# A memory mixer, eight experts and a feed-forward on one core: block-diagonal q built on the chip, weights loaded later, one more iteration between two layers

## The chip, the core and the metric

The kernel runs on one core of a Trainium2 chip. The time is in device microseconds (us) from the start of an execution to its end; a kernel's time is the median of its runs. TensorE does the matrix products, VectorE, ScalarE and GpSimd the elementwise work, SyncE issues most DMAs. In the rows they are PE (PEld: its weight loads), DVE, ACT, POOL and SP.

## The reference

Three stages follow each other: a recurrent mixer with a matrix memory (2 sequences of 768 tokens, 8 heads of 40), a mixture of 8 experts (each token goes to one, at most 384 per expert), and a feed-forward layer of 2048 with a PReLU. All numbers are float32.

```python
# mixer, for each t
m_new = np.maximum(f_gate[:, :, t] + m, i_gate[:, :, t])
f_stab = np.exp(f_gate[:, :, t] + m - m_new)
i_stab = np.exp(i_gate[:, :, t] - m_new)
C = f_stab[..., None, None] * C + i_stab[..., None, None] * np.einsum('bhd,bhe->bhde', vt, kt)
n = f_stab[:, :, None] * n + i_stab[:, :, None] * kt
h_tilde = np.einsum('bhde,bhe->bhd', C, qt)
nq = np.einsum('bhd,bhd->bh', n, qt)[:, :, None]
y[:, :, t] = sigmoid(o_gate[:, :, t]) * h_tilde / np.maximum(np.abs(nq), 1.0)
# experts: x is (1536, 320), w1 (8, 320, 1024), w2 (8, 1024, 320)
logits = x @ w_gate                      # the largest picks the expert
h = np.maximum(np.einsum('ecd,edf->ecf', disp, w1), 0.0)
y = np.einsum('ecf,efd->ecd', h, w2)     # scaled by the gate's weight
# second feed-forward: w_in (320, 2048), w_out (2048, 320)
h = x @ w_in
g = np.maximum(h, 0.0) + alpha * np.minimum(h, 0.0)
out = g @ w_out
```

## The kernel before

**Mixer.** The recurrence is done in 12 chunks of 128 tokens (6 for each sequence), by a loop over chunks `i`; 0 to 9 run in the loop, 10 and 11 behind it, in code written out. For a chunk TensorE makes the scores k·q of all heads (`scores`, L393), the values (`values`, L456), the share of the state of earlier chunks (`inter`, L418), the new state (`update`, L427) and the router's logits. Two chunks share one load, a pair: `qk` (q and k with heads of three side by side on 120 partitions), `tk` (v and k by token) and `qbd`, a second copy of q in block-diagonal form, so that one product makes the scores of three heads. In `qbd` each of the three blocks of 40 partitions holds its own head's columns, and the rest is zero. The kernel zeroes both `qbd` buffers once (L251) and then writes each pair's blocks by three DMAs (`load_pair`, L264). Decays come back from DRAM as a tile `Gb` per chunk, are masked on GpSimd (`causal`, L379) and raised to e on ScalarE. GpSimd also weighs k by the decay (`weigh_k`, L402, tile `kw`), which `update` needs, multiplies the output gate (`gate`, L492, tile `rs`) and issues the indirect DMAs that scatter finished rows into the experts' slots (`scatter`, L639). The scores of chunk i + 1 stand in iteration i, right behind `update(i)`.

Weights of an expert come in four quarters; `load_quarter` (L179 to L181, tiles `w1r`, `w2r`) issues three DMAs for each. Those of expert 0 are loaded in the mixer, one in each iteration from `Z1` = 6.

**Experts.** Products keep float32's precision by splitting each operand into a high and a low part that TensorE multiplies at its faster rate: three matmuls in place of one. ScalarE writes the high part and VectorE or GpSimd the low one (L188). Expert `e` goes through 8 steps `f`: layer 1 (L938) into one of three banks `hps0`, `hps1`, `qs2`, whose numbers start anew with each expert, ReLU parts `gh`, `gl` (L1072, L1073), and layer 2 (L950 to L952) `LAG` = 2 steps later. Between them stand transposes of the next expert's x (at f = `XE` = 2, 3, 4; L924), the splitting of the next expert's weights, and steps that turn the float64 bits of the second feed-forward's weights into float32 (`cv` tiles, L976 to L982). At which `f` such a step stands is set by `SC`. An iteration ends in a branch on whether an expert has more than 256 tokens (L1169), in which the engines meet.

**Second feed-forward.** Groups of tokens (2, 2, 4 and 4 blocks of 128 in the first pass, three times 4 in the other three) go through four `f` of a pass: layer 1 into `hps`, ScalarE's two ReLUs and VectorE's sum (`ng`, `g`), the split into `g3h` and `g3l` one iteration later, and layer 2 two iterations later: `pend` holds the layer-2 steps that wait, and is emptied down to `LAG`. `XG` says at which `f` of a group the next group's x is transposed (`xtp`). More `cv` steps run in the first three passes.

The order on TensorE, VectorE, ScalarE and GpSimd is that in which the code is written; a scheduler orders SyncE's DMAs. All SyncE DMAs share one queue.

Of the kernel before, what the change touches and what calls it, by code (L numbers as in the profile page):

```python
# [19 lines left out]
P = 128  # L20
# [33 lines left out]
def kernel(  # L54
# [19 lines left out]
    nc = tc.nc  # L74
    _, B, _, NG, S = qks.shape
    NTB = tok.shape[1]
    D = 40
# [5 lines left out]
    r = DM - 2 * P  # L83
# [7 lines left out]
    SL = NBLK * P  # L91
# [2 lines left out]
    B0 = min(2, NBLK)  # L94
    N0 = B0 * P

    W1, W2, V7, V8, V9, NA, WA, WB, Z0, Z1, X0, LD, FL, XE, SC, SC0, F0, WC, LS, UO, DL, XG, LV, E0, S0, CUT = 12, 4, 0, (((0, 0, 0, 0), (1, 1, 1, 1), (2, 2, 2, 2), (2, 2, 2, 2)), ((1, 2, 2, 3), (1, 2, 2, 3), (1, 2, 2, 3)), ((1, 2, 2, 3), (1, 2, 2, 3), (0, 0, 0, 0)), ((0, 0, 0, 0), (0, 0, 0, 0), (0, 0, 0, 0))), ({0: (2, 3), 1: (4, 5), 2: (6, 7)}, {0: (8, 9), 1: (10, 11)}, {}), 6, 0, 6, 3, 6, 3, 3, (2, 1, 2, 4, 1), 2, (1, 0, 0, 0, 0, 1, 0, 1), (0, 0, 0, 0, 0, 0, 1, 1), {5: [0], 6: [1], 7: [2]}, 0, 1, 1, 4, ({2: (0, 2), 3: (1,)}, {1: (0,), 2: (2,), 3: (1,)}, {1: (0,), 2: (2,), 3: (1,)}), 3, 2, 0, (2, 3, 3, 3, 3, 3, 3, 0)
    QF = 2 * P
    NQ = F // QF
    cp = ctx.enter_context(tc.tile_pool(name="cp", bufs=1))  # L100
# [12 lines left out]
    def after(inst, anchor):  # L113

        tc.add_manual_dep(
            inst.ins, anchor.ins.name, mybir.DependencyInfo(mybir.DependencyClass.Sync, mybir.DependencyReason.DATA),
            reason="paced transfer",
        )
# [18 lines left out]
    def x_tiles(pool, n, i):  # L137
        t = [[pool.tile([P, n], F32R, name=f"x{i}{k}{x}", bufs=1) for x in "hl"] for k in range(3)]

        nc.gpsimd.memset(t[2][1][r:].bitcast(U32), 0)  # L140
        return t

    xq = x_tiles(xk, SL, 0)


    RING = 2 * NQ
# [85 lines left out]
    with ExitStack() as actx:  # L232
# [15 lines left out]
        qbds = []  # L248
        for x in range(2):
            qbds.append(ap.tile([P, 3 * NG, PB], F32, tag=f"qbd{x}", name=f"qbd{x}"))  # L250
            nc.gpsimd.memset(qbds[x], 0.0)  # L251
        ins, sgs = {}, {}

        def load_pair(i2, anchor=None, late=None):
            b, c2 = divmod(i2, NC // 2)
            sl = slice(c2 * PB, (c2 + 1) * PB)
            qk = rp.tile([3 * D, 2, NG, PB], F32, tag="qk", name="qk")
            d = nc.sync.dma_start(out=qk[:, 1 if i2 == 0 else slice(0, 2)], in_=qks[:, b, 1 if i2 == 0 else slice(0, 2), :, sl])
            if i2 and anchor is not None:
                after(d, anchor)  # L260
            qbd = qbds[i2 % 2]
            for j in range(3):
                n = 3 if j < 2 else 2
                d = nc.sync.dma_start(  # L264
                    out=qbd[j * D:(j + 1) * D].rearrange("p (g j) s -> p g j s", j=3)[:, :n, j, :],
                    in_=qks[j * D:(j + 1) * D, b, 0, :n, sl],
                )
                if i2 < 2:
                    after(d, anchor)
            tk = rp.tile([P, 2, tok.shape[2]], F32, tag="tk", name="tk")  # L270
            d = nc.sync.dma_start(out=tk, in_=tok[:, 2 * i2:2 * i2 + 2, :])
            if anchor is not None:
                after(d, late or anchor)
            if i2 == 0:
                after(nc.sync.dma_start(out=qk[:, 0], in_=qks[:, b, 0, :, sl]), late)
            for x in range(2):
                cs = slice(x * P, (x + 1) * P)
                v1t = tk[:, x, :H * D1].rearrange("p (h d) -> p h d", h=H)
                ktt = tk[:, x, H * D1:H * D1 + DM].rearrange("p (h d) -> p h d", h=H)
                ins[2 * i2 + x] = (qk[:, 0, :, cs], qk[:, 1, :, cs], qbd[:, :, cs], v1t, ktt)  # L280
# [335 lines left out]
        def adv(g, n):  # L616

            for _ in range(n):
                next(by_start[g], None)
# [95 lines left out]
        for i in range(LB):  # L715
# [15 lines left out]
            if Z0 <= i < Z0 + 4:  # L731
                n = NS // P // 4
                rows = disp.rearrange("(a p) d -> p a d", p=P)[:, (i - Z0) * n:(i - Z0 + 1) * n, :]
                after(nc.sync.dma_start(out=rows, in_=zt[:, :DM].unsqueeze(1).to_broadcast([P, n, DM])), anchor[i - 1])
            if Z1 <= i < Z1 + NQ:
                load_quarter(0, i - Z1, anchor[i - 1])
            if i and ok(i + 1):
                decay(i + 1, range(4))
# [53 lines left out]
                nc.scalar.activation(sg1, sg1, AF.Sigmoid)  # L792
            if i % 2 and i // 2 + 2 < NTB // 2:
                load_pair(i // 2 + 2)
            if i == 7:
                after(nc.sync.dma_start(out=zt, in_=cst[:, C_ROW:]), anchor[i])
            ins.pop(i), Dt.pop(i), Pts.pop(i)
# [471 lines left out]
    sums = sp.tile([P, NTB, DM], F32, name="sums", bufs=1)  # L1269
    ghl3 = [[sp.tile([P, GN], F32R, name=f"g3{x}{i}", bufs=1) for x in "hl"] for i in range(3)]  # L1270

    def group_x(i0, nb, k):
        c0 = i0 % GB * P
        parts = [[t[:, c0:c0 + nb * P] for t in pair] for pair in xsets[i0 // GB]]
        ps = lambda k: pm.tile([P, 512], F32, tag="m", name="xtp")
        x_part(lambda m: sums[:, i0 + m, :], nb, ps, parts, k)
# [18 lines left out]
    for np0, gi in [(0, g) for g in range(len(FIRST))] + [(p, g) for p in (1, 2, 3) for g in range(len(OTHERS))]:  # L1295
# [4 lines left out]
        for f in range(f0, f1):  # L1300
# [45 lines left out]
                            nc.sync.dma_start(out=out[i * P:(i + 1) * P, :], in_=sums[:, i, :])  # L1346

            pend.append(l2step)
            while len(pend) > LAG:
                pend.pop(0)()  # L1350
            low_rows()
            convert(V8[np0][gi][f - f0])
# [77 lines left out]
```

## Time and profile before

| | us |
|---|---|
| median of 3 runs | 506.01 (502.34 to 509.98) |
| the profiled execution | 504.48 |
| its span, first to last instruction | 502.7 |
| TensorE busy | 454.7 (90%) |
| VectorE busy | 342.4 (68%) |
| ScalarE busy | 246.3 (49%) |
| GpSimd busy | 125.5 (25%) |
| mean granted TensorE clock | 0.925 |

The profile is of one execution; what lies around its span is 1.8 us. A TensorE that is busy is not at its peak: at a granted clock of 0.50 the same instruction takes up to twice as long. In the rows, a bracket such as [3.15 <-POOL kw L402] is the time for which the engine stood idle before the instruction, and what ended it. A timeline lists instructions in order of time (start, length, engine, line and operation). Windows list for each stretch its bounds and length, the busy time of PE, PEld, DVE, ACT and POOL, the granted clock, the DMA engines' busy share and the GB/s moved. Waits are grouped by the waiting instruction and what released it: total us, how many, the longest.

### The profile page before, as it was taken

What the parts mean: (1) busy time and instruction counts of PE and PEld (TensorE: products, weight loads), DVE (VectorE), ACT (ScalarE), POOL (GpSimd) and SP (SyncE); (2) the same over time, 40 slices, a digit from 0 to 9 for tenths busy, and PEclk for the clock granted to TensorE, in tenths of its full rate; (3) what the DMA queues carried; (4) which work ended last, traced back from release to release, by engine and by line L of the source; (5) the groups of instructions that cost most, each with busy time, mean ns of one, the idle gap of its engine ahead of it and who ended that gap; (6) DMA issues with size and microseconds to landing.
All of it is one profiled execution on the core that took longest, in us unless ns stands there. A gap on an engine that the chain in (4) does not pass through costs nothing. (4 is left out here: it accounts for less than half of the span.)

```text
span 502.7 us, 8039 instructions
## 1 busy us (share of the span) xinstructions
PE 454.7 (90%) x2800; PEld 408.0 (81%) x2800; DVE 342.4 (68%) x700; ACT 246.3 (49%) x558; POOL 125.5 (25%) x115
## 2 busy tenths in 40 slices
PE   5969998889879889796998898997999999999996
PEld 2658886787879889796998897895998898789995
DVE  7627683866788783859688224775889988764544
ACT  3446782525457544555556124562654454354442
POOL 4244325646534221423233224300000000000000
PEclk8759995966999999889899999997999999999999
DMA  6999999424786753657473003221221231000102
GB/s 190 263 278 337 351 317 253 147 78 133 241 254 197 222 175 88 212 155 244 147 220 94 22 1 103 74 84 42 73 59 53 57 101 52 2 0 1 52 20 86
DMA packets 42428, 68.86 MB, mean 137 GB/s; under 512 B 4383, under 2 KB 32354, under 8 KB 42383
## 3 DMA queue, kind: packets, MB, share of 16 engines
q1 hardware_dynamic: 41023, 64.18, 42.5%
q0 software_dynamic: 1152, 3.86, 2.4%
q8 instruction: 26, 0.43, 0.4%
q10 hardware_dynamic: 208, 0.24, 0.1%
q14 instruction: 19, 0.16, 0.1%
HBM read 56.49 MB, written 11.85 MB: 136 GB/s over the span
## 5 line engine op out<-in xcount | busy, mean ns | idle before, releaser
L188 POOL TENSOR_TENSOR w2l<-w2r,w2h 128x640 fp32r<-128x640 f32 x31 | 53.2, 1715 | 93.1 <-ACT w2h L224 77.8
L1316 DVE SCALAR_TENSOR_TENSOR g<-ng,nalt,g 128x512 f32<-128x512 f32 (+1 forms) x52 | 36.9, 709 | 47.5 <-ACT g L1315 47.4
L1314 ACT ACTIVATE ng<-hps 128x512 f32<-128x512 f32 (+1 forms) x52 | 29.4, 565 | 74.8 <-PE hps L938 73.3
L950 PE MATMUL acc<-w2h,gh 128*128 128x320 f32 x128 | 40.8, 319 | 4.9 <-DVEq L1169 4.9
L952 PE MATMUL acc<-w2h,gl 128*128 128x320 f32 x128 | 40.5, 316 | 1.6 <-DVE gl L1073 1.6
L951 PE MATMUL acc<-w2l,gh 128*128 128x320 f32 x128 | 40.4, 315 | 0.0
L1072 ACT ACTIVATE gh<-hps 128x256 fp32r<-128x256 f32 x50 | 19.1, 384 | 40.3 <-PE hps L938 38.5
L387 ACT ACTIVATE Gb<-Gb,bT 128x128 f32<-128x128 f32 x96 | 29.5, 388 | 12.3 <-POOL Gb L379 12.3
L188 DVE TENSOR_TENSOR w1h<-w1r,w1h 64x256 fp32r<-64x256 f32 x32 | 33.4, 1047 | 1.0
L188 DVE TENSOR_TENSOR g3l<-g,g3h 128x512 fp32r<-128x512 f32 (+1 forms) x52 | 33.5, 644 | 0.1
L1073 DVE SCALAR_TENSOR_TENSOR gl<-hps,gh 128x256 fp32r<-128x256 f32 x50 | 20.5, 421 | 18.6 <-ACT gh L1072 18.1
L952 PE MATMUL acc<-w2h,g3l 128*128 128x320 f32 x96 | 30.3, 316 | 2.4 <-DVE g3l L188 2.3
L952 PE MATMUL acc<-wouth,g3l 128*128 128x320 f32 x96 | 30.8, 321 | 0.3 <-DVE g3l L188 0.3
L950 PE MATMUL acc<-wouth,g3h 128*128 128x320 f32 x96 | 30.7, 320 | 0.1
L1319 ACT CAST g3h<-g 128x512 fp32r<-128x512 f32 (+1 forms) x52 | 30.6, 589 | 0.3 <-DVE g L1316 0.3
L951 PE MATMUL acc<-woutl,g3h 128*128 128x320 f32 x96 | 30.6, 319 | 0.0
L950 PE MATMUL acc<-w2h,g3h 128*128 128x320 f32 x96 | 29.8, 310 | 0.8 <-ACT g3h L1319 0.8
L456 PEld LDWEIGHTS Ops<-tk,Pt 128*128 128x128 f32 x192 | 26.7, 217 | 4.2 <-issue 2.6
L393 PE MATMUL qs<-qbd,qk 120*128 120x384 f32 (+1 forms) x72 | 30.1, 567 | 0.0
L951 PE MATMUL acc<-w2l,g3h 128*128 128x320 f32 x96 | 29.6, 309 | 0.0
L950 PEld LDWEIGHTS acc<-w2h,gh 128*128 128x128 f32 x128 | 25.1, 196 | 5.4 <-issue 3.8
L1315 ACT ACTIVATE g<-hps 128x512 f32<-128x512 f32 (+1 forms) x52 | 29.2, 561 | 0.0
(334 smaller groups left out, 1384.0 us busy)
## 6 DMA issues: line engine op xcount, KB each, us to landing
w2r<-w SPq DMA_DIRECT2D x32, 320.0 KB
w1r<-w SPq DMA_DIRECT2D x32, 256.0 KB
Gb<-gd SPq DMA_DIRECT2D x12, 512.0 KB
raw<-wout SPq DMA_DIRECT2D x8, 640.0 KB
raw<-win SPq DMA_DIRECT2D x8, 512.0 KB
tk<-tok SPq DMA_DIRECT2D x6, 648.0 KB
disp<-zt SPq DMA_DIRECT2D x4, 960.0 KB
qk<-qks SPq DMA_DIRECT2D x5, 720.0 KB
```

What stands on the lines that cost most here:

```text
L188: eng.tensor_tensor(out=out, in0=a, in1=b.bitcast(F32), op=ALU.subtract)
L387: nc.scalar.activation(Dt[i][:, h, :], Dt[i][:, h, :], AF.Exp, bias=bT[:, c, b * H + h:b * H + h + 1])
L393: nc.tensor.matmul(ps[:, :nh * P].rearrange("p (h t) -> p h t", h=nh), kst[:nh * D, g, :], qbd[:nh * D, h0:h0 + nh, :], start=True, stop=True,
L456: nc.tensor.matmul(Opss[i][:, h, :], Pts[i][:, h, :], v1t[:, h, :], start=True, stop=True)
L950: nc.tensor.matmul(a, gh[:, ms], wh, start=first, stop=False)
L951: nc.tensor.matmul(a, gh[:, ms], wl, start=False, stop=False)
L952: nc.tensor.matmul(a, gl[:, ms], wh, start=False, stop=last)
L1073: nc.vector.scalar_tensor_tensor(out=gl, in0=ps, scalar=0.0, in1=gh.bitcast(F32), op0=ALU.max, op1=ALU.subtract)
L1314: nc.scalar.activation(ng, ps, AF.Relu, scale=-1.0)
L1315: nc.scalar.activation(g, ps, AF.Relu)
L1316: nc.vector.scalar_tensor_tensor(out=g, in0=ng, scalar=nalt[:, f:f + 1], in1=g, op0=ALU.mult, op1=ALU.add)
L1319: nc.scalar.copy(gh, g)
```

## The change

It has five parts.

1. From the second pair on, `qbd` is no longer written by DMAs. `spread_q` makes it from the q part of `qk`: each of the three blocks is q times a column of 0 and 1 (`bd`), two blocks on GpSimd (120 x 3 x 256 each), one on ScalarE (120 x 2 x 256). It stands at the end of each even iteration i, for the pair of chunks i + 2 and i + 3. The zeroing of the second buffer goes.
2. Expert 0's weight quarters are loaded in iterations 7 and 8 (`Z1`), and quarters 2 and 3 behind the loop.
3. `XE` goes from 2 to 3, and `SC` from (1,0,0,0,0,1,0,1) to (1,0,1,0,0,0,1,0).
4. In the second feed-forward a fourth pair of `g3` tiles is laid over expert x's tile, which is dead by then, and layer 2 runs three iterations behind layer 1.
5. The last entry of `XG`: the last group's x is transposed one `f` earlier.

```diff
-    W1, W2, V7, V8, V9, NA, WA, WB, Z0, Z1, X0, LD, FL, XE, SC, SC0, F0, WC, LS, UO, DL, XG, LV, E0, S0, CUT = 12, 4, 0, (((0, 0, 0, 0), (1, 1, 1, 1), (2, 2, 2, 2), (2, 2, 2, 2)), ((1, 2, 2, 3), (1, 2, 2, 3), (1, 2, 2, 3)), ((1, 2, 2, 3), (1, 2, 2, 3), (0, 0, 0, 0)), ((0, 0, 0, 0), (0, 0, 0, 0), (0, 0, 0, 0))), ({0: (2, 3), 1: (4, 5), 2: (6, 7)}, {0: (8, 9), 1: (10, 11)}, {}), 6, 0, 6, 3, 6, 3, 3, (2, 1, 2, 4, 1), 2, (1, 0, 0, 0, 0, 1, 0, 1), (0, 0, 0, 0, 0, 0, 1, 1), {5: [0], 6: [1], 7: [2]}, 0, 1, 1, 4, ({2: (0, 2), 3: (1,)}, {1: (0,), 2: (2,), 3: (1,)}, {1: (0,), 2: (2,), 3: (1,)}), 3, 2, 0, (2, 3, 3, 3, 3, 3, 3, 0)
+    W1, W2, V7, V8, V9, NA, WA, WB, Z0, Z1, X0, LD, FL, XE, SC, SC0, F0, WC, LS, UO, DL, XG, LV, E0, S0, CUT = 12, 4, 0, (((0, 0, 0, 0), (1, 1, 1, 1), (2, 2, 2, 2), (2, 2, 2, 2)), ((1, 2, 2, 3), (1, 2, 2, 3), (1, 2, 2, 3)), ((1, 2, 2, 3), (1, 2, 2, 3), (0, 0, 0, 0)), ((0, 0, 0, 0), (0, 0, 0, 0), (0, 0, 0, 0))), ({0: (2, 3), 1: (4, 5), 2: (6, 7)}, {0: (8, 9), 1: (10, 11)}, {}), 6, 0, 6, 3, 7, 3, 3, (2, 1, 2, 4, 1), 3, (1, 0, 1, 0, 0, 0, 1, 0), (0, 0, 0, 0, 0, 0, 1, 1), {5: [0], 6: [1], 7: [2]}, 0, 1, 1, 4, ({2: (0, 2), 3: (1,)}, {1: (0,), 2: (2,), 3: (1,)}, {0: (0,), 1: (2,), 2: (1,)}), 3, 2, 0, (2, 3, 3, 3, 3, 3, 3, 0)
...
-            nc.gpsimd.memset(qbds[x], 0.0)
-        ins, sgs = {}, {}
+        nc.gpsimd.memset(qbds[0], 0.0)
+        ins, sgs, q_of = {}, {}, {}
+
+        def spread_q(i2):
+
+            qbd = qbds[i2 % 2][:3 * D].rearrange("p (g j) s -> p g j s", j=3)
+            for j in range(3):
+                n = 3 if j < 2 else 2
+                if j < 2:
+                    nc.gpsimd.tensor_scalar_mul(qbd[:, :n, j, :], q_of[i2][:, :n, :], bd[:, j:j + 1])
+                else:
+                    nc.scalar.activation(qbd[:, :n, j, :], q_of[i2][:, :n, :], AF.Copy, scale=bd[:, j:j + 1])
...
-            for j in range(3):
+            q_of[i2] = qk[:, 0]
+            for j in range(3 if i2 == 0 else 0):
...
-            if Z1 <= i < Z1 + NQ:
+            if Z1 <= i < Z1 + 2:
                 load_quarter(0, i - Z1, anchor[i - 1])
...
+            if i % 2 == 0 and i // 2 + 1 < NTB // 2:
+                spread_q(i // 2 + 1)
...
+        for q in range(2, NQ):
+            load_quarter(0, q, anchor[i - 1])
...
+    ghl3.append([xqs[:, i * GN:(i + 1) * GN] for i in range(2)])
+
...
-            while len(pend) > LAG:
+            while len(pend) > len(ghl3) - 1:
                 pend.pop(0)()
```

SyncE's queue in the second half of the mixer, before: `disp` is the last of four fills of the experts' slots with zeros, the `Gb` are decays, `tk` belongs to chunks 8 and 9, the `qbd` and the second `qk` to chunks 10 and 11.

```order
L258 DMA qk<-qks 120x6x256
L734 DMA disp<-zt 128x6x320
L179 DMA w1r_93<-w 128x2x256
L180 DMA w1r_93<-w1t 64x256
L181 DMA w2r_95<-w 128x640
L374 DMA Gb<-gd 128x1024
L271 DMA tk<-tok 128x1296
L179 DMA w1r_93<-w 128x2x256
L180 DMA w1r_93<-w1t 64x256
L181 DMA w2r_96<-w 128x640
L264 DMA qbd_136<-qks 40x3x256 x2
L264 DMA qbd_136<-qks 40x2x256
```

The same place now:

```order
L270 DMA qk<-qks 120x6x256
L746 DMA disp<-zt 128x6x320
L386 DMA Gb<-gd 128x1024
L283 DMA tk<-tok 128x1296
L181 DMA w1r_88<-w 128x2x256
L182 DMA w1r_88<-w1t 64x256
L183 DMA w2r_90<-w 128x640
L386 DMA Gb<-gd 128x1024
L810 DMA zt<-cst 128x384
L181 DMA w1r_88<-w 128x2x256
L270 DMA qk<-qks 120x6x256
```

The first quarter of weights now stands behind `tk` of chunks 8 and 9, and the `qbd` loads are gone.

GpSimd in iterations 6 to 8 of the mixer, before (`AFFINE_SELECT` is `causal`, `rs` the gate, and the DMA is a scatter):

```order
L379 AFFINE_SELECT Gb<-Gb 128x1024
L492 TENSOR_TENSOR rs<-sg_161,rec 128x320
L402 TENSOR_TENSOR kw<-tk,Gb 128x320
L379 AFFINE_SELECT Gb<-Gb 128x1024
L492 TENSOR_TENSOR rs<-sg_408,rec 128x320
L402 TENSOR_TENSOR kw<-tk,Gb 128x320
L639 DMA disp<-xt,si 3072x320
```

The same place now:

```order
L391 AFFINE_SELECT Gb<-Gb 128x1024
L504 TENSOR_TENSOR rs<-sg_155,rec 128x320
L414 TENSOR_TENSOR kw<-tk,Gb 128x320
L262 TENSOR_SCALAR qbd_129<-qk,ct 120x3x256 x2
L391 AFFINE_SELECT Gb<-Gb 128x1024
L504 TENSOR_TENSOR rs<-sg_399,rec 128x320
L414 TENSOR_TENSOR kw<-tk,Gb 128x320
L651 DMA disp<-xt,si 3072x320
```

Two multiplications stand behind `kw` of the odd chunk, and ahead of the next mask, gate and `kw`.

VectorE in expert 3, from `gl` of f = 2 to `gl` of f = 6, before: `x00l` to `x02l` are the low parts of the next expert's x, `w1l` and `w1h` those of its weights, `woutl` and `cv` a step of the conversion.

```order
L1073 SCALAR_TENSOR_TENSOR gl_1423<-qs_72,gh_1422 128x256
L188 TENSOR_TENSOR x00l<-qs_70,x00h 128x384
L1073 SCALAR_TENSOR_TENSOR gl_1419<-hps_1430,gh_1418 128x256
...
L1073 SCALAR_TENSOR_TENSOR gl_1423<-qs_72,gh_1422 128x256
L188 TENSOR_TENSOR w1l_109<-w1r_93,w1h_101 128x512
L188 TENSOR_TENSOR w1h_101<-w1r_93,w1h_101 64x256
L188 TENSOR_TENSOR woutl_1391<-cv_1387,wouth_1390 128x640
L976 TENSOR_SCALAR cv_1386<-raw_1384 128x768
L977 TENSOR_SCALAR cv_1386<-cv_1386 128x768
L1073 SCALAR_TENSOR_TENSOR gl_1419<-hps_1430,gh_1418 128x256
```

The same place now:

```order
L1089 SCALAR_TENSOR_TENSOR gl_1417<-qs_72,gh_1416 128x256
L190 TENSOR_TENSOR w1l_102<-w1r_88,w1h_94 128x512
L190 TENSOR_TENSOR w1h_94<-w1r_88,w1h_94 64x256
L190 TENSOR_TENSOR woutl_1385<-cv_1381,wouth_1384 128x640
L992 TENSOR_SCALAR cv_1380<-raw_1378 128x768
L993 TENSOR_SCALAR cv_1380<-cv_1380 128x768
L1089 SCALAR_TENSOR_TENSOR gl_1413<-hps_1424,gh_1412 128x256
...
L190 TENSOR_TENSOR xq<-qs_70,xq 64x384
L190 TENSOR_TENSOR w1l_104<-w1r_88,w1h_96 128x512
L190 TENSOR_TENSOR w1h_96<-w1r_88,w1h_96 64x256
L1089 SCALAR_TENSOR_TENSOR gl_1413<-hps_1424,gh_1412 128x256
```

The conversion step moved from f = 5 to f = 2, and the x parts from f = 2, 3, 4 to f = 3, 4, 5.

## Rows read from the trace of the kernel before

**Rows 1.** Busy time in three windows: mixer, experts, second feed-forward.

```profile
0.00:126.00 126.00, 110.26 (x616) 90.01 (x617) 80.12 (x252) 64.34 (x189) 56.43 (x64) 0.78 0.79 235
126.00:304.00 178.00, 159.12 (x1167) 153.11 (x1165) 123.78 (x215) 87.37 (x182) 58.75 (x42) 0.97 0.52 160
304.00:503.00 199.00, 185.31 (x1021) 164.87 (x1021) 138.50 (x235) 94.56 (x187) 10.35 (x10) 0.97 0.18 54
```

**Rows 2.** Timeline of TensorE in the mixer.

```profile
30.72 1.45 PE L427 MATMUL Ups<-tk,kw 128*120 128x123 f32 x6 [4.15 <-POOL kw L402]
...
31.96 3.70 PE L393 MATMUL qs<-qbd,qk 120*128 120x384 f32 x6
...
44.81 1.93 PE L393 MATMUL qs<-qbd,qk 120*128 120x384 f32 x6
...
77.72 1.45 PE L427 MATMUL Ups<-tk,kw 128*120 128x123 f32 x6 [3.15 <-POOL kw L402]
```

**Rows 3.** Busy time in a window behind that last wait.

```profile
77.70:90.30 12.60, 12.58 (x50) 11.11 (x51) 5.16 (x16) 3.92 (x14) 6.54 (x7) 0.50 1.01 265
```

**Rows 4.** Timeline of GpSimd in the mixer.

```profile
40.54 0.73 POOL L402 TENSOR_TENSOR kw<-tk,Gb 128x320 f32<-128x320 f32 x1
...
46.84 1.08 POOL L379 TENSOR_SCALAR_AFFINE_SELECT Gb<-Gb 128x1024 f32<-128x1024 f32 x1
...
76.93 0.73 POOL L402 TENSOR_TENSOR kw<-tk,Gb 128x320 f32<-128x320 f32 x1 [6.52 <-DMA tk<-tok]
...
117.29 1.28 POOL L595 TENSOR_SCALAR spots<-zt,sf 128x384 fp32r<-128x384 f32 x1 [1.38 <-DVE mv L561]
```

**Rows 5.** Timeline of SyncE's issues in the mixer.

```profile
66.59 0.38 SPq L271 DMA_DIRECT2D tk<-tok  x1
...
72.13 2.18 SPq L264 DMA_DIRECT2D qbd<-qks  x3
```

**Rows 6.** Busy time in two windows of the mixer.

```profile
45.00:60.00 15.00, 15.00 (x92) 12.98 (x91) 9.18 (x31) 9.73 (x28) 5.76 (x8) 0.89 1.05 342
...
90.00:105.00 15.00, 12.44 (x94) 11.02 (x94) 13.27 (x45) 6.75 (x21) 8.55 (x10) 0.96 0.22 79
```

**Rows 7.** TensorE's waits in the expert stage, by releaser.

```profile
PE hps L938 <- DVE gl L1073: 7.9, 8, 2.9
...
PE acc L950 <- DVEq L1169: 4.9, 2, 3.5
```

**Rows 8.** Timeline of VectorE at the end of expert 3.

```profile
205.35 1.68 DVE L188 TENSOR_TENSOR w1h<-w1r,w1h 64x256 fp32r<-64x256 f32 x1
...
208.40 1.77 DVE L977 TENSOR_SCALAR cv<-cv 128x768 f32<-128x768 f32 x1
...
211.46 0.42 DVE L188 TENSOR_TENSOR w1h<-w1r,w1h 64x256 fp32r<-64x256 f32 x1
```

**Rows 9.** Timeline of TensorE there, first layer 1 of expert 4.

```profile
210.55 0.58 PE L938 MATMUL hps<-x00h,w1h 128*128 128x256 f32 x1 [2.91 <-DVE gl L1073]
```

**Rows 10.** Busy time in the window behind that wait.

```profile
210.00:215.00 5.00, 4.45 (x19) 4.45 (x20) 2.74 (x7) 1.10 (x2) 0.00 (x0) 0.50 0.44 122
```

**Rows 11.** TensorE's waits in the second feed-forward, by releaser.

```profile
PE hps L938 <- DVE w2l L188: 3.5, 2, 2.9
PE acc L952 <- DVE g3l L188: 2.6, 6, 0.9
```

**Rows 12.** Busy time in windows of the second feed-forward.

```profile
332.00:344.00 12.00, 8.39 (x50) 7.06 (x48) 9.50 (x16) 5.45 (x10) 0.00 (x0) 0.95 0.19 56
344.00:348.40 4.40, 4.40 (x15) 4.21 (x16) 2.01 (x3) 1.59 (x3) 0.00 (x0) 0.50 0.00 0
...
365.00:445.00 80.00, 76.88 (x419) 67.70 (x418) 69.08 (x115) 39.73 (x73) 0.00 (x0) 1.00 0.17 50
```

**Rows 13.** Timeline of TensorE at the start of the second feed-forward.

```profile
311.02 0.55 PE L924 MATMUL xtp<-ct,sums 128*128 128x128 f32 x3 [1.05 <-DMA sums<-yd,gidx]
```

**Rows 14.** Timeline of GpSimd beside rows 8.

```profile
204.96 1.79 POOL L188 TENSOR_TENSOR w2l<-w2r,w2h 128x640 fp32r<-128x640 f32 x1 [1.86 <-PE hps L938]
```

More of the change, by code (lines that the diff above doesn't have):

```diff
@@ L141, in x_tiles @@
         return t
-    xq = x_tiles(xk, SL, 0)
+    xqs = xk.tile([P, 6 * SL], F32R, name="xq")
+    xq = [[xqs[:, (2 * k + i) * SL:(2 * k + i + 1) * SL] for i in range(2)] for k in range(3)]
+    nc.gpsimd.memset(xq[2][1][r:].bitcast(U32), 0)
     RING = 2 * NQ
@@ L267, in load_pair @@
                 )
-                if i2 < 2:
-                    after(d, anchor)
+                after(d, anchor)
             tk = rp.tile([P, 2, tok.shape[2]], F32, tag="tk", name="tk")
```

## The prediction

> **What bounds the kernel now.** I read the windows first, one for each stage. TensorE is busy for 110.3 of 126 us in the mixer, for 159.1 of 178 in the experts and for 185.3 of 199 in the second feed-forward, and no other engine comes near [rows 1]. So TensorE bounds every stage, and a change of this kind can win in two ways: by idle time of TensorE, which is 48 us in all, and by its clock, which was granted at 0.78 in the mixer and at 0.97 in the two others. The mixer is the odd one: its DMA engines are busy for 79% of it, against 52% and 18%, and in a window in the middle they are saturated (a share of 1.05 at 342 GB/s), while a window nearer the end has 0.22 [rows 6]. Then I read the timeline of TensorE for its long waits. In the mixer two of them end with `kw`, 4.15 us before `update(2)` and 3.15 before `update(8)` [rows 2]. Last, the waits by releaser, for the two later stages [rows 7, 11].
>
> **Part 1 and 2, the mixer.** The wait of 3.15 us comes from a late load: GpSimd stood idle for 6.52 us for `tk` of chunks 8 and 9 before `kw` at 76.93 [rows 4], and that load had been issued at 66.59 [rows 5], 10.3 us earlier. Ahead of it in the queue stood a quarter of weights: 128 x 512, 64 x 256 and 128 x 640 numbers of 4 bytes are 0.66 MB, 2 to 3 us at the 235 to 342 GB/s of the windows. After the change that quarter stands behind `tk`. The `qbd` copies go as well: 40 x 8 x 256 numbers of 4 bytes, 0.33 MB or 1.0 to 1.4 us a pair, 5 to 7 us of a saturated stretch for five pairs, and an issue of 2.18 us on SyncE for each [rows 5]. I expect `kw` some 5 us earlier, so the 3.15 go. Behind that wait lie 12.6 us at a granted clock of 0.50 with TensorE busy throughout [rows 3]. How little that is shows in one product: the six scores matmuls of a chunk took 3.70 us at 31.96, where the clock had fallen, and 1.93 at 44.81, where TensorE had been running on [rows 2]. At full clock the 12.6 would be 6.3. The wait and its clock are worth 3.15 + 6.3 = 9.4.
>
> The wait of 4.15 has another cause: decays `Gb` of chunk 2 that queue behind the first loads. They land about 1.4 us earlier without `qbd`, but `scores(2)` now waits for multiplications that stand behind `kw(1)`; I put the two against each other and take nothing.
>
> What the multiplications cost is the unknown. GpSimd does two per pair, of 120 x 768 elements, and no row has that form. The nearest are a select of 128 x 1024 at 1.08 us and a multiplication by a column, 128 x 384 at 1.28 [rows 4]. In proportion to the columns that is 0.8 us by the one and 2.6 by the other. I take 1.3, nearer to the select, as the short one holds more than its columns. They are hidden while they fit between `kw` of the odd chunk and `scores` of the next even one: `kw(3)` ends at 41.27 [rows 4] and `scores(4)` starts at 44.81 [rows 2], so 3.5 us cover 2 x 1.3 = 2.6. At 2.6 each the pair takes 5.1 us, and TensorE waits 1.6. ScalarE's third block, 120 x 512, runs beside them; its busy time is 64 of 126 us [rows 1]. The product must also find its `qk` landed, and for the last pair that is tight: `qk` of chunks 10 and 11 now stands behind two quarters of weights, and a late one would hold GpSimd and ScalarE, which take their instructions in order, `causal`, `gate` and `kw` behind it with them. I deduct 2 us for all of this. The later quarters fall into the stretch with a DMA share of 0.22 [rows 6]; I count nothing for them. Part 1 and 2 together: 9.4 - 2.0 = **7.4**, between 0 (another load or a multiplication takes the place of the wait) and 11 (the first wait shrinks by 1.4 as well, and nothing is deducted).
>
> A rule of the Trainium skill bears on the multiplication: "GPSIMD Engine Reference", section "4.1 Engine selection", has one-input elementwise work on GpSimd at roughly line rate. The select's row agrees with that, the 1.28 for 384 columns does not. By the rule the 2 us would not be deducted and the sum would be 2 us larger.
>
> **Part 3, the experts.** Layer 1 waits for `gl` for 7.9 us in 8 places, the longest 2.9 [rows 7]. That one is the first product of expert 4 [rows 9]. It writes a bank that `gl` of the seventh step of expert 3 must have read, two steps earlier only, since the banks are numbered anew. And that `gl` stands on VectorE behind a conversion step: `woutl`, two `cv`, 1.77 us for the longer one, after a `w1h` of 1.68 [rows 8]. The change moves the step from f = 5 to f = 2, and in its place come x parts, which cost about 0.5 each. So the 2.9 should go, and with it the clock: the 5 us behind it ran at 0.50 with 4.45 us of work [rows 10], which is 2.2 too much. The other waits of the group are 5.0 us at seven places; where an expert carries a step at f = 5 the same argument holds, and I take a quarter, 1.2. The two waits for the branch (4.9 us, [rows 7]) come behind the step at f = 0, which stays. Sum 2.9 + 2.2 + 1.2 = 6.3, I take **6.2**; bounds 2.9 (the wait alone) and 10.1 (all 7.9 and the clock).
>
> **Part 4 and 5, the second feed-forward.** Layer 1 waits for 3.5 us in two places [rows 11]. They lie in the window from 332 to 344, where TensorE is busy for 8.4 of 12 us while VectorE is busy for 9.5, and the 4.4 us behind them run at a clock of 0.50 [rows 12]: x parts of the last group of the first pass stand on VectorE just before the group that needs them. One `f` earlier, they have a whole step more: 3.5 + 2.2 = 5.7. The third iteration covers layer 2's waits for `g3l`, 2.6 us in 6 places, of which I take 2.0; in the window from 365 to 445 VectorE is busy for 86% of the time and TensorE for 96%, so what the extra iteration buffers is unevenness, not a bound. Against it, at the start layer 2 of the first group no longer fills the time in which the next rows are gathered: TensorE waited 1.05 there [rows 13], and I add 1.3. Sum 5.7 + 2.0 - 1.3 = **6.4**, bounds 3.5 and 8.
>
> **The sum.** 7.4 + 6.2 + 6.4 = 20.0. The profiled execution took 504.5, so 484.5. It is 1.5 below the median of the three runs, and I add that: **486**. With all upper bounds, 29, it is 477; with all lower ones, 0 + 2.9 + 3.5 = 6.4, it is 499.6.
>
> **Rivals.** (1) *GpSimd becomes the mixer's bound, and the kernel is slower.* If a multiplication takes 3 us, the two exceed their cover of 3.5 by 2.5, for five pairs 12.5 us, and at least three of these waits would throw the clock down as the one of rows 3 did, 3 x 6.3 = 19. Part 1 then costs 12.5 + 19 - 9.4 = 22 us, against 12.6 from the other stages: 504.5 + 9.5 + 1.5 = 515. With the three slow stretches the break-even is near 4.1 us for a pair of multiplications, without them near 7.9. For it: rows 4's 1.28 for a short one, and GpSimd and VectorE slow each other: a `w1h` of 64 x 256 took 1.68 us while a GpSimd subtraction ran from 204.96 to 206.75 [rows 14], and 0.42 us at 211.46 [rows 8]. Against it: the select. The Trainium skill, "SBUF — State Buffer", section "SBUF: two separate sides", calls the pair of ports that the two share an exclusive lock, held for a whole instruction, not a division of bandwidth; it speaks against this change, since VectorE is at work for 80 us of the mixer. The trace agrees for two-input operations, as the 1.68 against 0.42 show; no row here has VectorE beside a one-input multiplication on GpSimd. (2) *The wait in the mixer only moves*: to the last `qk`, to scatters, to the weights of expert 0 that now come last. Then parts 1 and 2 give 0 and the time is 486 + 7.4 = 493. (3) *VectorE bounds the later stages*, and work moved on it is paid elsewhere: experts 2, second feed-forward 2, 486 + 8.6 = 495. For it: 9.5 of 12 us busy [rows 12]; against it: the stage means are 70% [rows 1]. (4) *Nearly nothing is won*, because several of these hold: 501.
>
> **Chances and range.** The forecast has 0.50 (480 to 492), rival (1) 0.07, (2) 0.16, (3) 0.15, (4) 0.12. The range of 8 in 10 goes from 475, just under the sum of the upper bounds, to 499, that of the lower ones; it leaves out rivals (1) and (4) for the most part. Two per cent, about what a measurement of this kernel can tell from no change (its three runs spread over 7.6 us), is 496 here: faster 0.75, within it 0.18, slower 0.07.
>
> **What would show it.** In the changed profile: `update(8)` without a wait for `kw` and a granted clock near 1 from 78 to 90; GpSimd's two multiplications at 0.8 to 1.8 us each, and `scores` of even chunks without a wait for them; the first product of expert 4 without a wait for `gl`; no wait of layer 1 near 340 and no slow 4 us behind it; fewer waits of layer 2 for `g3l`. Wrong would make it: multiplications of 2.5 us or more; half-clock stretches that show up behind other waits, since the clock is half of the sum (6.3 + 2.2 + 2.2 of 20); or VectorE's waits growing where the moved work lands.

## The result, and the profile after

The changed kernel took 488.0 us (487.2 to 489.6, 3 runs) against 506.0 before (502.3 to 510.0): a ratio of 0.968, 95% interval 0.958 to 0.979, so it is faster by 18 us of median. The profiled execution took 488.0, its span 486.2. In the second group of experiments the same kernel took 501.8 (4 runs) against 512.0 (19 runs), a ratio of 0.982 (0.972 to 0.992). Ratios are made of undisturbed executions (in the second group the 4 fastest of the 19 of the kernel before), medians of all; the profiles of two kernels below (e3 and e7) are of disturbed ones, and of these the second feed-forward is read above all.

I divide the span at two landmarks that every variant has: the first product of expert 0 (`hps`, layer 1), and the first product with `first_slots` behind the last branch of the experts; the third window ends with TensorE's last product. First the windows between them and one inside the mixer, before (length, busy PE, PEld, DVE, ACT, POOL, granted clock, DMA share, GB/s):

```profile
0.00:125.27 125.27, 109.53 (x609) 89.28 (x610) 80.09 (x251) 63.68 (x188) 55.81 (x63) 0.78 0.79 234
125.27:273.74 148.47, 131.02 (x952) 126.26 (x951) 114.18 (x191) 80.60 (x163) 52.98 (x36) 0.97 0.61 188
273.74:498.84 225.10, 214.13 (x1240) 192.45 (x1240) 147.50 (x258) 101.99 (x208) 16.74 (x17) 0.98 0.16 49
30.00:60.00 30.00, 29.28 (x178) 25.24 (x178) 17.99 (x58) 20.01 (x63) 12.91 (x16) 0.85 1.03 320
```

The same windows after, and four more:

```profile
0.00:122.14 122.14, 104.51 (x609) 83.04 (x610) 81.05 (x251) 66.84 (x193) 76.20 (x72) 0.85 0.73 227
122.14:268.13 145.99, 130.18 (x953) 125.04 (x952) 114.26 (x191) 80.23 (x164) 53.23 (x36) 0.98 0.64 191
268.13:482.41 214.28, 208.97 (x1240) 189.80 (x1240) 146.92 (x258) 102.48 (x208) 16.58 (x17) 0.99 0.17 51
30.00:60.00 30.00, 27.82 (x140) 23.47 (x141) 12.72 (x39) 13.84 (x45) 19.00 (x16) 0.69 0.75 228
60.00:90.00 30.00, 27.38 (x202) 24.04 (x202) 24.16 (x74) 22.81 (x67) 24.84 (x21) 1.00 0.87 272
322.00:345.00 23.00, 23.00 (x128) 20.23 (x127) 20.93 (x35) 15.52 (x30) 0.00 (x0) 1.00 0.24 72
345.00:470.00 125.00, 124.85 (x694) 112.42 (x693) 95.49 (x158) 62.98 (x116) 0.00 (x0) 1.00 0.14 43
```

The mixer is 3.1 us shorter, the experts 2.5, the second feed-forward 10.8; together 16.4. The mixer's gain is not idle time: TensorE stood idle for 15.7 us there before and for 17.6 after. It is clock, 0.85 against 0.78. TensorE's waits in the mixer after, by releaser (total, how many, longest):

```profile
PE qs L405 <- POOL qbd L262: 5.1, 4, 2.9
PE Ups L439 <- POOL kw L414: 2.9, 1, 2.9
```

Four waits for GpSimd's multiplications stand where one of the two for `kw` was [rows 2]. In time, TensorE and GpSimd:

```profile
32.18 3.78 PE L405 MATMUL qs<-qbd,qk 120*128 120x384 f32 x6 [2.92 <-POOL qbd L262]
...
75.99 1.99 PE L405 MATMUL qs<-qbd,qk 120*128 120x384 f32 x6 [1.35 <-POOL qbd L262]
...
81.38 0.76 PE L439 MATMUL Ups<-tk,kw 128*120 128x123 f32 x6
```

```profile
43.02 4.81 POOL L262 TENSOR_SCALAR qbd<-qk,ct 120x768 f32<-120x768 f32 x2
...
77.64 0.73 POOL L414 TENSOR_TENSOR kw<-tk,Gb 128x320 f32<-128x320 f32 x1
```

`update(8)` at 81.38 waits for nothing and has 0.76 us in place of 1.45, and the window from 60 to 90 ran at 1.00; behind the old wait it was 0.50 [rows 3]. Its `kw`, at 77.64, no longer waits for `tk`, but begins no earlier than before (76.93 [rows 4]): GpSimd and TensorE were late by then, after a stretch from 30 to 60 at a clock of 0.69, against 0.85 before. The two multiplications of a pair take 4.8 us, 2.4 each; the five pairs lie between 4.4 and 4.8.

In the experts the waits after are

```profile
PE hps L954 <- DVE gl L1089: 6.8, 9, 1.5
PE acc L966 <- DVEq L1185: 6.6, 2, 3.5
PE qs L954 <- DVE gol L1089: 0.9, 1, 0.9
```

The 2.9 for `gl` is gone as forecast, and as much has come back elsewhere: 7.9 + 4.9 us before [rows 7] are 6.8 + 6.6 now, 0.6 more. In the second feed-forward what is left stands at its start:

```profile
PE xtp L940 <- issue: 2.2, 1, 2.2
PE xtp L940 <- DMA sums<-yd,gidx: 1.0, 1, 1.0
PE qs L1151 <- DMA xd<-yd,gidx: 0.8, 1, 0.8
PE hps L954 <- DVE w2l L190: 0.8, 1, 0.8
```

From 345 to 470 TensorE is idle for 0.15 of 125 us, at full clock; before it had idled for 3.1 of 80 in a like stretch [rows 12].

### The profile page after: what moved, and what is told of

Same layout as the page of the kernel before. It is cut to its first block, busy times and chain, and to the rows that moved or that the text cites. A ratio compares the mean times of both kernels' runs of the same rounds, so it can differ in the third digit from the quotient of the medians.

```text
span 486.2 us, 8022 instructions
## 1 busy us (share of the span) xinstructions
PE 443.7 (91%) x2800; PEld 397.9 (82%) x2800; DVE 342.9 (71%) x700; ACT 249.6 (51%) x563; POOL 146.0 (30%) x124
## 5 line engine op out<-in xcount | busy, mean ns | idle before, releaser
L1088 ACT ACTIVATE gh<-hps 128x256 fp32r<-128x256 f32 x50 | 19.1, 385 | 45.2 <-PE hps L954 43.6
L190 DVE TENSOR_TENSOR w1h<-w1r,w1h 64x256 fp32r<-64x256 f32 x32 | 29.8, 932 | 0.9
L405 PEld LDWEIGHTS qs<-qbd,qk 120*128 120x128 f32 (+1 forms) x72 | 15.3, 229 | 17.5 <-POOL qbd L262 5.7
L468 PEld LDWEIGHTS Ops<-tk,Pt 128*128 128x128 f32 x192 | 24.7, 203 | 4.5 <-DVE t L486 1.4
L954 PE MATMUL hps<-xq,w1h 128*128 128x256 f32 x144 | 25.6, 295 | 2.2 <-DVE gl L1089 2.2
L468 PE MATMUL Ops<-tk,Pt 128*128 128x41 f32 x192 | 24.5, 290 | 1.9 <-DVE t L486 1.2
L190 DVE TENSOR_TENSOR w1l<-w1r,w1h 128x512 fp32r<-128x512 f32 x29 | 25.3, 872 | 1.1 <-DVEq L1185 0.5
L209 ACT CAST w1h<-w1r 128x768 fp32r<-128x768 f32 x31 | 25.7, 829 | 0.0
L190 DVE TENSOR_TENSOR g3l<-g,g3h 128x512 fp32r<-128x512 f32 (+1 forms) x39 | 25.1, 642 | 0.0
L967 PEld LDWEIGHTS acc<-w2l,gh 128*128 128x128 f32 x128 | 24.9, 194 | 0.0
L968 PEld LDWEIGHTS acc<-w2h,gl 128*128 128x128 f32 x128 | 24.6, 192 | 0.0
## 6 DMA issues: line engine op xcount, KB each, us to landing
Gb<-gd SPq DMA_DIRECT2D x12, 512.0 KB, 6.7
raw<-win SPq DMA_DIRECT2D x8, 512.0 KB, 4.5
```

The lines of the kernel that those rows point to most:

```text
L190: eng.tensor_tensor(out=out, in0=a, in1=b.bitcast(F32), op=ALU.subtract)
L209: copy(hi, a)
L405: nc.tensor.matmul(ps[:, :nh * P].rearrange("p (h t) -> p h t", h=nh), kst[:nh * D, g, :], qbd[:nh * D, h0:h0 + nh, :], start=True, stop=True,
L468: nc.tensor.matmul(Opss[i][:, h, :], Pts[i][:, h, :], v1t[:, h, :], start=True, stop=True)
L954: nc.tensor.matmul(ps, a, b_, start=j == 0 and 0 in ks, stop=j == len(seq) - 1 and 1 in ks)
L967: nc.tensor.matmul(a, gh[:, ms], wl, start=False, stop=False)
```

## The experiments

Each chip ran the kernel before beside the variants: 509.8 us in the first group (19 runs), 512.0 in the second (19), 510.9 in the third (7). That is 4 to 6 us above the runs shown ahead, so I compare within a group, and read stages in the profiles.

**Parts 1 and 2 alone (e1), part 3 alone (e2), parts 4 and 5 alone (e3).** e1 is the changed kernel with the other parts undone, e2 and e3 are the kernel before with theirs done:

```diff
# e1, from the changed kernel
-..., 3, (1, 0, 1, 0, 0, 0, 1, 0), ..., {0: (0,), 1: (2,), 2: (1,)}), ...
+..., 2, (1, 0, 0, 0, 0, 1, 0, 1), ..., {1: (0,), 2: (2,), 3: (1,)}), ...
-    ghl3.append([xqs[:, i * GN:(i + 1) * GN] for i in range(2)])
# e2, from the kernel before
-..., 2, (1, 0, 0, 0, 0, 1, 0, 1), ...
+..., 3, (1, 0, 1, 0, 0, 0, 1, 0), ...
# e3, from the kernel before (the lines that make expert x one tile are left out)
-..., {1: (0,), 2: (2,), 3: (1,)}), ...
+..., {0: (0,), 1: (2,), 2: (1,)}), ...
+    ghl3.append([xqs[:, i * GN:(i + 1) * GN] for i in range(2)])
```

> The kernel before with parts 1 and 2 alone (block-diagonal q on the chip, later weight loads). By the landmarks of the two traces the first product of expert 0 came 3.1 us earlier with the whole change, so by theory A (the mixer's gain is eaten by GpSimd's multiplications, 2.2 to 2.4 us each, above all the first pair's) this kernel is 3 us faster than before, within 2, and expert 0 starts near 122. By theory B (the mixer gave the 7.4 of the prediction and a later stage took it back) it is 7 us faster and expert 0 starts near 118.

> The kernel before with part 3 alone (x parts an iteration later, conversion steps at other f). By theory A (the wait of 2.9 us and its slow clock go, but a wait for a branch in expert 2 grows by about 1.8 and brings a slow clock of its own) it is 2.5 us faster, within 2, and the time from the first product of expert 0 to the last branch falls from 148.5 to 146. By theory B (the 6.2 of the prediction, hidden by a chance of the one trace) it is 6 us faster.

> The kernel before with parts 4 and 5 alone (third iteration between layers, last group's x earlier). By theory A (nearly all of the gain is here, since both the waits and the slow stretches behind them go) it is 10 to 11 us faster. By theory B (6.4 as predicted, and the rest of what the trace shows in this stage came from an earlier start of other work) it is 6 to 7 us faster.

Measured: e1 508.8 us (10 runs), ratio 0.999 (0.995 to 1.003); e2 506.3 (10), 0.995 (0.990 to 1.000); e3 499.9 (4), 0.973 (0.962 to 0.984). The three ratios add up to 3.3%, near the 3.2% of the whole change's 0.968 (0.982 in the second group). In e1 expert 0 starts at 121.0, near the 122 of theory A, but the end shows nothing of it: its expert stage took 153.4 us against 148.5 in the profile before, with the same code. Its ten runs show no gain either, and only one of them has a profile, so what the mixer's 4 us are worth in time is not shown. So one stage can differ by 5 us and more between two executions, and that had to be found first (below). e3 is theory A's: nearly all of the gain is in the second feed-forward.

**The first pair by DMA (e4).** In the changed kernel `qbd` of chunks 2 and 3 is loaded again (and its buffer zeroed again, left out here):

```diff
...
-            for j in range(3 if i2 == 0 else 0):
+            for j in range(3 if i2 < 2 else 0):
...
-            if i % 2 == 0 and i // 2 + 1 < NTB // 2:
+            if i and i % 2 == 0 and i // 2 + 1 < NTB // 2:
```

> The changed kernel, but the block-diagonal q of chunks 2 and 3 is loaded by DMA as before; GpSimd makes it from chunks 4 and 5 on. By theory A (the first pair's multiplications cost 5.6 us: scores of chunk 4 came at 50.4 in place of 44.8, through a wait of 2.9 us and a clock of 0.69 from 30 to 60) it is 4 to 5 us faster than the changed kernel, and scores of chunk 4 are back near 45. By theory B (the copies in the queue bring back the wait for kw of chunk 2, and the slow clock starts there anyway) it is the same as the changed kernel within 1.5 us.

It took 493.6 us (4 runs), ratio 0.973 (0.966 to 0.981). Scores of chunk 4 came at 45.5 and expert 0 at 121.6. But e1, whose mixer is that of the changed kernel, also has chunk 4 at 45.5 and expert 0 at 121.0. Theory A falls: the late chunk 4 of the profile after is not what the first pair costs for good. Its wait only changed its name (4.3 us for `kw` in e4).

**The changed kernel again (e9), and which executions differ.**

> The changed kernel once more, on the chip on which its variants run. If the slow clock from 30 to 50 us in its first profile was that execution's alone, as the kernel with parts 1 and 2 (scores of chunk 4 at 45.5 with the same mixer) says, scores of chunk 4 come near 45.5 here and a slow stretch lies elsewhere in the mixer, with expert 0 still starting at 121 to 122. If it belongs to the changed kernel, they come near 50 again.

It took 501.8 us (4 runs), on the same chip as e5, e7 and e8. Chunk 4 came at 49.6, as in the first profile; so the slow clock from 30 to 50 came in two of the three profiles of this mixer, and expert 0 started at 121.0, 122.1 and 123.9 in the three. The 15.8 us between the two profiled executions of one kernel lie mostly in the experts, in the work on the third block of expert 2. After, in the first profile, and then in e9, whose landmarks come 2 us later:

```profile
184.00:202.00 18.00, 17.11 (x136) 17.05 (x137) 9.51 (x23) 7.91 (x19) 3.46 (x2) 1.00 0.41 130
```

```profile
186.00:204.00 18.00, 17.06 (x77) 16.96 (x77) 3.97 (x13) 2.42 (x9) 0.00 (x0) 0.55 0.05 17
```

TensorE's products there, in the first profile after and in e9:

```profile
184.89 0.44 PE L954 MATMUL qs<-xq,w1h 128*128 128x128 f32 x2 [0.93 <-DVE gol L1089]
185.17 0.28 PE L954 MATMUL qs<-xq,w1l 128*128 128x128 f32 x1
185.28 0.61 PE L954 MATMUL qs<-xq,w1h 128*128 128x128 f32 x4
```

```profile
187.04 0.44 PE L954 MATMUL qs<-xq,w1h 128*128 128x128 f32 x2 [0.94 <-DVE gol L1089]
187.32 0.27 PE L954 MATMUL qs<-xq,w1l 128*128 128x128 f32 x1
187.43 0.81 PE L954 MATMUL qs<-xq,w1h 128*128 128x128 f32 x4
```

The same instructions behind the same wait, and in one execution the clock falls to half in the middle of them and stays there to the end of the block: 18 us at 0.55 lose 8 us. This stretch is in five of the fourteen profiles, with the old schedule of part 3 (e1, e3, e7) and with the new one (e9, e13). With that known, the stages of all profiles (a star marks that stretch):

| kernel | mixer | experts | second feed-forward |
|---|---|---|---|
| before | 125.3 | 148.5 | 225.1 |
| e2, part 3 | 126.1 | 147.6 | 226.4 |
| e8, part 5 | 124.0 | 146.8 | 221.9 |
| e7, part 4 | 126.4 | 153.8* | 224.4 |
| e3, parts 4, 5 | 126.1 | 153.7* | 216.8 |
| e1, parts 1, 2 | 121.0 | 153.4* | 227.4 |
| after | 122.1 | 146.0 | 214.3 |
| e9, after again | 123.9 | 155.5* | 218.7 |
| e4, first pair by DMA | 121.6 | 146.9 | 216.6 |
| e10, doubled multiplications | 149.3 | 147.5 | 216.5 |
| e5, selects | 119.1 | 146.6 | 217.1 |
| e13, selects again | 123.8 | 153.6* | 216.7 |
| e11, selects, part 3 undone | 119.5 | 147.3 | 216.5 |
| e12, selects, step at f = 1 | 122.8 | 137.1 | 216.7 |

Without parts 1 and 2 the mixer takes 125.6 us on the mean of five, with them (e1, after, e9, e4) 122.2: 3.4. Without the starred ones the experts take 147.5 by the old schedule (before, e8, e11) and 146.9 by the new one (e2, after, e4, e5, e10): 0.6. The second feed-forward takes 226.3 without parts 4 and 5 (before, e2, e1) and 216.7 with both (nine profiles): 9.6. Together 13.6.

**Part 4 alone (e7) and part 5 alone (e8).** Each is the kernel before with one of e3's two edits.

> The kernel before with part 4 alone (the third iteration between layers). Both parts together shortened the second feed-forward from 226 to 216 us (three profiles with them, three without). By theory A, the prediction's split, part 4 gives 1 us net and part 5 the larger share: the waits of layer 1 for x parts near 340 and the slow stretch behind them stay, and the stage takes 224 us or more. By theory B (the deeper queue gives VectorE an iteration to catch up everywhere, there too) part 4 alone takes most of those waits away, and the stage is at 219 or below.

> The kernel before with part 5 alone (the last group's x an f earlier). By theory A the waits of 3.6 us near 340 and the slow 4.4 us behind them go, and the stage takes 219 to 221 us; the waits of layer 2 for g3l (2.6 us) stay. By theory B the wait only moves to the next work that VectorE is late with, and the stage stays at 224 us or more.

e7 took 509.1 us (10 runs), ratio 0.988 (0.981 to 0.996); e8 505.1 (10), 1.000 (0.994 to 1.006). In the profiles the stage takes 224.4 with part 4 and 221.9 with part 5, 1.9 and 4.4 less than without, and 9.6 less with both. The waits show what each leaves; e7, then e8:

```profile
PE hps L940 <- DVE w2l L190: 3.7, 2, 2.9
```

```profile
PE acc L952 <- DVE g3l L188: 2.7, 6, 0.9
...
PE hps L938 <- DVE w2l L188: 1.0, 1, 1.0
```

Part 4 takes the waits for `g3l` and leaves that for the last group's x with its slow clock; part 5 does the reverse. Theory A's mechanism holds in both. Its sizes leave 3.3 us of the whole open, but that the two are worth more together is not shown: the stage took 214.3 and 218.7 us in two profiles of the changed kernel, and e7's clock there was 0.97 against 0.99 with both.

**Selects in place of multiplications (e5, and e13 as a control).**

```diff
-                if j < 2:
-                    nc.gpsimd.tensor_scalar_mul(qbd[:, :n, j, :], q_of[i2][:, :n, :], bd[:, j:j + 1])
+                if j != 1:
+                    nc.gpsimd.affine_select(
+                        out=qbd[:, :n, j, :], in_=q_of[i2][:, :n, :], pattern=[[0, n], [0, PB]], compare_op=ALU.is_ge, fill=0.0,
+                        base=D - 1 if j == 0 else -2 * D, channel_multiplier=-1 if j == 0 else 1,
+                    )
```

> The changed kernel, but GpSimd makes its two blocks of each pair (the first and the third) by a select that keeps the block's partitions and writes 0 elsewhere, and ScalarE makes the second. By theory A (the form of the instruction sets GpSimd's time: 128 x 1024 took 1.08 us as a select, 128 x 384 took 1.28 as a multiplication by a column) the two take about 1.4 us a pair in place of 4.4 to 4.8, the four waits for them (5.1 us in all) fall under 1.5, and expert 0 starts 2 to 5 us earlier than with the changed kernel. By theory B (the number of elements, or VectorE beside it, sets the time) the pair still takes 3 us or more and nothing moves by more than 1 us.

> The variant with GpSimd's selects once more, as the control of this call. Its mixer ends near 119, its second feed-forward takes 215 to 218 us, and the expert stage 146 to 147, or 8 more if the slow clock hits expert 2, as it did in four of the ten profiles so far, with and without part 3.

```profile
26.93 1.41 POOL L262 TENSOR_SCALAR_AFFINE_SELECT qbd<-qk 120x768 f32<-120x768 f32 x2
```

```profile
0.00:119.10 119.10, 108.20 (x609) 87.85 (x610) 78.56 (x251) 67.64 (x193) 60.87 (x72) 0.80 0.77 232
```

Theory A: the two selects take 1.4 to 1.7 us a pair, the waits for `qbd` are gone from e5's list, and TensorE idles for 10.9 us in the mixer (119.10 - 108.20), 6.7 less than in the profile after. But the mixer is 119.1, 123.8, 119.5 and 122.8 us long in the four profiles with selects, 121.3 on the mean, only 0.9 less than with multiplications: at a clock of 0.77 to 0.83 against 0.82 to 0.85 most of what the waits gave went to the clock. The two sets overlap (121.0 to 123.9 with multiplications), and e13, the same kernel as e5, missed its 119 by 4.7, so no gain in the mixer's length is shown. e5 took 487.3 us (4 runs; ratio 0.961, 0.951 to 0.972) beside 501.8 of e9 on the same chip, e13 498.5 (0.979, 0.968 to 0.989) on another. Of the 15.5 us between the profiled executions of e5 and e9, 8.9 lie in the experts, in the starred stretch, which e9 and e13 have and e5 has not.

**Multiplications twice (e10).** Each of GpSimd's multiplications is issued twice (`for _ in range(2):` ahead of it); the results are the same.

> The changed kernel with each of GpSimd's multiplications issued twice (the second writes the same numbers again), so that a pair takes some 9 us in place of 4.4 to 4.8. By theory A (GpSimd's multiplications stand on the path of scores from the second pair on, as the four waits of 5.1 us in all say) each of the five pairs adds its 4.5 us less what slack there is, the waits for block-diagonal q come to 18 to 25 us and expert 0 starts at 138 to 145. By theory B (GpSimd has slack of a pair's length, and the waits of the changed kernel are those of the first pair alone) they stay under 10 us, and expert 0 starts before 130.

```profile
PE qs L406 <- POOL qbd L263: 21.4, 5, 7.5
```

```profile
47.64 9.27 POOL L263 TENSOR_SCALAR qbd<-qk,ct 120x768 f32<-120x768 f32 x4
```

518.9 us in one run: theory A, but expert 0 came at 149.3, later than the 138 to 145 expected. 4.5 us more per pair, 22.5 in all, made 16.3 us more of these waits and a mixer 27 longer than after: TensorE idled for 11.6 us more in all, and its products took 15.6 more, at a clock of 0.73. This is rival (1) of the prediction, built: with 9 us a pair the change was slower than before (505.9 to 513.9 in the seven runs beside it).

**Part 3 undone, and the step of f = 0 moved (e11, e12).** Both from e5:

```diff
# e11
-..., 3, (1, 0, 1, 0, 0, 0, 1, 0), ...
+..., 2, (1, 0, 0, 0, 0, 1, 0, 1), ...
# e12
-..., 3, (1, 0, 1, 0, 0, 0, 1, 0), ...
+..., 3, (0, 1, 1, 0, 0, 0, 1, 0), ...
```

> The variant with GpSimd's selects, with part 3 undone (x parts and conversion steps at the old f). By theory A (part 3 is worth 1 us at most: where no slow clock hits expert 2, the expert stage took 146.8 and 148.5 us without it and 146.0 to 147.6 with it) it is the same as the select variant of this call within 3 us, and the idle time of TensorE in the stage is 17.4 against 16.4. By theory B (the 6.2 of the prediction) it is 6 us slower, through the wait of 2.9 us and the slow clock behind it.

> The variant with GpSimd's selects, with the conversion step of f = 0 moved to f = 1, where it stands behind the branch of the expert before. By theory A (the two long waits that part 3 left, 3.2 and 3.5 us at a branch, wait for the step of f = 0 on VectorE) both fall under 1.5, the slow stretches behind them go, and the expert stage takes 140 to 143 us where no slow clock hits expert 2. By theory B (VectorE's work is only moved, and layer 1 waits for gl as much more) the stage stays at 146 or above.

e11 took 498.0 us (4 runs), e13 beside it 498.5, and e11's experts 147.3: theory A, part 3 is worth next to nothing. e12 took 481.6 (477.1 to 482.8, 4 runs), ratio 0.942 (0.931 to 0.953), the best of all kernels here. Its experts, then the waits in them:

```profile
122.79:259.95 137.16, 127.16 (x953) 122.08 (x951) 115.71 (x191) 80.21 (x164) 52.29 (x35) 1.00 0.67 203
```

```profile
PE hps L957 <- DVE gl L1092: 6.8, 9, 1.5
PE acc L971 <- DVE gl L1092: 1.6, 1, 1.6
PE qs L1202 <- DVEq L1188: 0.7, 1, 0.7
PE qs L957 <- DVE gol L1092: 0.2, 1, 0.2
```

The two waits at branches, 6.6 us after, are gone and nothing took their place; the clock is 1.00 throughout, where in the profile after the 5 us behind each wait ran at 0.66 and 0.67. The stage is 9.8 us shorter than with part 3 (137.1 against 146.9), below the 140 to 143 of theory A. It is one profile, but all four runs lie below the eight of e11 and e13 (488.8 to 503.6). VectorE did the same work; it only came behind the branch at which the engines meet.

## Why the prediction was right in its sum and not in its parts

The time, 488.0, is 2.0 us from the forecast; the sum of the terms was 20.0, the profiles give 13.6 by the stage means and 16.4 by the two executions compared. No term was near: 7.4, 6.2 and 6.4 were forecast, 3.4, 0.6 and 9.6 measured. That the first result lay so near has luck in it: in the second group the change gave 10.2 us of median, and its 501.8 lies above the range, on a chip where the kernel before takes 512.

*Mixer.* The step "the 3.15 go, and the clock behind them" held: `update(8)` waits for nothing, and 60 to 90 ran at 1.00 (0.78 before). `kw` came the forecast 5 us earlier in e1 and e4 (72.1 and 72.0) and no earlier in the profile after. The step that was mis-sized is "I take 1.3, nearer to the select": a multiplication took 2.2 to 2.4, near the 2.6 of the row of the same form, which the prediction had as its upper bound. The four waits for it are 5.1 us, against the 2 deducted, and 3 of these are the first pair, whose wait I had set against an earlier `Gb` and taken as nothing: of the 4.15 for `kw` 2.92 stayed, 2.92 for `qbd` came on top, and the clock from 30 to 60 was 0.69 against 0.85. That clock does not always follow: in e1, behind the same wait of 2.9 for `qbd`, it was 0.92. (The 4.15 stands before `update(1)`; the prediction calls it `update(2)`, and no sum rests on that.) A pair of 4.4 to 4.8 us lies above rival (1)'s break-even of 4.1, which supposed slow stretches behind the later waits too; from 60 to 90 there were none. The same-form row was the better one, by the engine's own kind of instruction and not by its size. A tight `qk` of the last pair and late weights did not show.

The Trainium skill, "GPSIMD Engine Reference", section "4.1 Engine selection", puts one-input work on GpSimd at about line rate. The runs here agree for the select (0.7 us for 768 columns, 0.9 ns each) and not for the multiplication by a column (2.2 to 2.4 for the same 768), so the measurement decides. Nor did VectorE cause it: from 43.6 to 47.3, for most of the 4.8 us pair, VectorE had no instruction.

*Experts.* The term failed, and the step is "the two waits for the branch come behind the step at f = 0, which stays": it stayed, but its wait did not. In expert 2 it grew from 1.43 to 3.18, and not by chance: it is 1.35 to 1.44 in all six profiles with the old schedule and 3.14 to 3.18 in all seven with the new one. TensorE there, before and after:

```profile
167.94 0.38 PE L950 MATMUL acc<-w2h,gh 128*128 128x320 f32 x1 [1.43 <-DVEq L1169]
```

```profile
164.48 0.50 PE L966 MATMUL acc<-w2h,gh 128*128 128x320 f32 x1 [3.18 <-DVEq L1185]
```

From `w1l` on VectorE has the same instructions ahead of that branch in both kernels, with one `gl` in another place; what changed is what GpSimd was doing beside it. VectorE before, then after, then GpSimd after:

```profile
161.43 1.47 DVE L188 TENSOR_TENSOR w1l<-w1r,w1h 128x512 fp32r<-128x512 f32 x1
...
166.57 0.49 DVE L977 TENSOR_SCALAR cv<-cv 128x640 f32<-128x640 f32 x1
```

```profile
156.23 2.00 DVE L190 TENSOR_TENSOR w1l<-w1r,w1h 128x512 fp32r<-128x512 f32 x1
...
161.90 1.71 DVE L993 TENSOR_SCALAR cv<-cv 128x640 f32<-128x640 f32 x1
```

```profile
156.10 1.58 POOL L190 TENSOR_TENSOR w2l<-w2r,w2h 128x640 fp32r<-128x640 f32 x1 [0.85 <-ACT w2h L226]
161.48 1.78 POOL L190 TENSOR_TENSOR w2l<-w2r,w2h 128x640 fp32r<-128x640 f32 x1 [3.79 <-ACT w2h L226]
```

`w1l` took 0.5 us more and `cv` 1.2 more, together 1.75, which is the growth of the wait. Each began 0.1 and 0.4 us after a GpSimd subtraction and ended 0.5 and 0.4 us after it. This is what the Trainium skill's "SBUF — State Buffer", section "SBUF: two separate sides", says of the shared ports, a lock held for a whole instruction; the trace agrees for `w1l`, which has two inputs. For `cv`, with one, the section asks for a mode of VectorE that no view here shows. In the prediction I used it for the mixer alone, where it did not matter. The other half of the term, the slow clock behind the 2.9 wait, is real in the profile before but was worth 2.2 us in one execution; a like stretch came behind the grown wait (5 us at 0.66, at 1.00 before), and the starred stretch, 8 us, comes with either schedule. Rival (3), that work moved on VectorE is paid elsewhere, had given the experts 2 us; it holds for this stage and not for the next.

*Second feed-forward.* The mechanism was right and the size was not: 6.4 forecast, 9.6 measured. The waits near 340 and the slow clock behind them went, the start waits 1.5 us longer (2.2 + 1.0 against 0.6 + 1.1; 1.3 was forecast). The term "third iteration, 2.0" was too small: it counted the waits for `g3l` by name, while the stretch behind 345 lost nearly all its idle time, 3.4 us with those for `g3h`. Nor is the clock's share of 2.2 enough: of the 10.8 us between the two profiles 5.7 are idle time of TensorE and 5.2 shorter busy time, of the same products. The 3.3 us that neither part gives alone are not settled by one profile of each.

What stays open: why the clock fell in expert 2 in five executions and not in nine, behind the same instructions and, within one schedule, the same wait (1.3 us by the old one, 0.9 by the new). e12's profile has no such stretch and its four runs lie within 6 us; whether its shorter wait of 0.2 us ahead of that block prevents it, or chance, was not tried.

## What to carry to other kernels

Price a new instruction by the nearest row of its own form, not by one of its size: a select and a multiplication of the same engine differ by three times here. Where engines meet at a branch, put bulk work behind it and not ahead: moving one step by one iteration was worth 10 us in the one profile of it, more than the whole of part 3, which had moved another. And before a stage's gain is put down to an edit, look at the same stage in a kernel whose edit is elsewhere: here untouched code differed by 7 us, through clock alone.

## What the runs showed of the hardware

The same products behind the same wait of 0.9 us ran on at a granted clock of 1.00 in one execution and at 0.55 for 18 us in another. Idle time that was removed from a stretch in which the clock falls again and again gave little back here: with selects the mixer had 5 us less idle time than with multiplications (11.1 against 16.1 on the mean of four profiles each) and was 0.9 us shorter, less than two profiles of one kernel differ by, while 11.6 us more of idle time made it 27 longer in the one profile of that. A VectorE subtraction of 128 x 512 that began 0.1 us behind a GpSimd subtraction took 2.00 us, and one of the same form with GpSimd idle 0.68.
